# Splitting two of the 51 loads of a scan input into a 120-row and an 8-row transfer

## The chip, the cores and the metric

The kernel runs on one core of one Trainium2 chip. A core has five engines with instruction streams of their own: TensorE (PE in the profile; PEld is its weight load), VectorE (DVE), ScalarE (ACT), GpSimd (POOL) and SyncE (SP), which here does nothing but issue transfers. Transfers between HBM and the on-chip memory (SBUF, 128 rows called partitions) are carried out by 16 DMA engines. The metric is the device time of one execution in microseconds (us); the profile shows the span from the first to the last instruction of one execution, which is somewhat shorter than the device time.

## The reference, cut to what matters

`a` and `b` have shape (8, 6400, 128). A linear recurrence runs along the 6400 steps of each of the 8 sequences, and its result is the input of a mixture of eight low-rank adapters, of which each row uses the best two:

```python
def _attn_ref(a, b):                 # a, b: (8, 6400, 128) float32
    h = zeros((8, 128))
    for t in range(6400):
        h = a[:, t] * h + b[:, t]
        out[:, t] = h
    return out

def _moe_ref(x, w_gate, A, B):       # x: (51200, 128); 8 adapters of rank 16
    logits = x @ w_gate
    topk = the 2 largest of the 8 logits of each row
    w = softmax over these 2
    delta = sum over the 2 of  w * ((x @ A[e]) @ B[e])
    return x + delta
```

Nothing of `a`, `b` or the result can be left in HBM: 26.2 MB of `a`, 26.2 MB of `b` and 26.2 MB of the result pass the DMA engines once each.

## The kernel before

The 51,200 rows are cut into 100 units of 512 rows. For each unit PE transposes `a` and `b` into PSUM, ACT copies the transposed `a` to SBUF, and DVE runs the recurrence as one scan instruction into `xT`. PE then forms the gate logits and the rank-128 products of all adapters (`ZL`), ACT copies them out (`zl`), a chain of small steps on POOL, DVE and ACT computes the gate weights, POOL or DVE multiplies (`zw`), PE transposes back (`T`), applies the second factor and adds x (`D`), and ACT copies the unit to `outt` (`oev`), from where SP stores it. A planner in Python fixes the order of instructions on each engine at build time and sets the waits on semaphores.

A transfer is planned by `add_dma`. Each issue in `starts` adds 16 to the semaphore of its slot when it has landed, and a user waits for the sum of all of them:

```python
def add_dma(name, eng, unit, starts, slot, ns, deps=(), kind="dma", issue=450.0, after=2000.0):
    if slot not in dma_sem:
        dma_sem[slot] = [sb(nc.semaphore(...)), 0]
    dma_sem[slot][1] += 16 * len(starts)
    sem, value = dma_sem[slot]

    def emit(h):
        for dst, src in starts:
            last = h.dma_start(dst, src).then_inc(sem, 16)     # line 429
        return last

    add(name, eng, kind, unit, issue * len(starts), emit, deps, (sem, value, ns, after))
```

`a` and `b` have rings of 8 places in SBUF, and a place holds two units: 128 partitions of 8 consecutive rows of 128 numbers, so 4 KB in a partition and 512 KB in a load. Three loads at the start and one at the end hold one unit alone (256 KB). The place `n` of `a` holds the units 2n-1 and 2n.

```python
def load(t, w):
    n = place(t, w)[0]                       # a: (w + 1) // 2,  b: w // 2
    many = 1 if (t, w) in alone else 2
    dst, i = rings[t][:, n % RING, :], QI    # RING = 8, QI = 8
    ...
    src = rows_of[t][w * UT : (w + many) * UT, :].rearrange("(p i) d -> p (i d)", i=i)
    add_dma(
        f"ld{t}{w}", "sp", ...,
        [(dst, src)],                        # one transfer of 128 partitions
        (t, n % RING, many, w if many == 1 else 0),
        1290.0 if many == 2 else 690.0,
        users.get((t, n - RING), []),        # PE has read what the place held before
    )
```

A store takes two units as well (512 KB), except the first two and the last two. It waits for the two copies to `outt` and for the scan 20 units later; the ring `outt` has 24 units.

```python
def o_evac(v):
    ...                                       # ACT (the last 8 units: ACT or DVE)
    copy(outt[:, v % NOUT, :], bank(("O", v))[:, :])     # line 978; after D{v} and store of v - 24

stores = [(u, 2) for u in range(0, NU - 2, 2)] + [(NU - 2, 1), (NU - 1, 1)]
def store(j):
    ...
    add_dma(f"st{j}", "sp", u0 + HOLD, [(rows, tile)], ("o", s0, n), ns,
            [f"oev{v}" for v in range(u0, u0 + n)] + [f"scan{min(u0 + HOLD, NU - 1)}"])
```

All loads of `a` and `b` and all stores are issued by SP, one after the other, on one queue (q1 in the profile).

Of the kernel before, what the change touches and what calls it, by code (L numbers as in the profile page):

```python
# [10 lines left out]


CFG = {
    "ring": 8,
    "xr": 20,
    "zr": 48,
# [263 lines left out]
def bass_associative_scan_2x2__then__mixture_of_adapters_kernel(  # L280
# [18 lines left out]
    NU = N // UT  # L299
    RING = CFG["ring"]  # L300
    XR = CFG["xr"]
    NOUT = CFG["nout"]
    HOLD = CFG["hold"]
    NAS = CFG["ast"]
    NZW, NZT = 3, 3
    ZR = CFG["zr"]
    TAIL = CFG["tail"]
# [61 lines left out]
    with ExitStack() as stack:  # L369
# [50 lines left out]
        def add_dma(name, eng, unit, starts, slot, ns, deps=(), kind="dma", issue=450.0, after=2000.0):  # L420

            if slot not in dma_sem:
                dma_sem[slot] = [sb(nc.semaphore("q_" + "_".join(map(str, slot)))), 0]
# [5 lines that stand above are left out]
                    last = h.dma_start(dst, src).then_inc(sem, 16)  # L429
                return last  # L430

            add(name, eng, kind, unit, issue * len(starts), emit, deps, (sem, value, ns, after))
# [163 lines left out]
        def place(t, w):  # L596

            shift = 1 if t == "a" else 0
            half = 64 * ((w + shift) % 2)
            return (w + shift) // 2, slice(half, half + 64)  # L600
# [7 lines left out]
        def column(t, w):  # L608

            return w * UT if t == "b" else 0  # L610

        def load(t, w):

            n = place(t, w)[0]
            many = 1 if (t, w) in alone else 2
            dst, i = rings[t][:, n % RING, :], QI
            if many == 1:
                dst, i = dst[:, column(t, w) : column(t, w) + UT], Q
            src = rows_of[t][w * UT : (w + many) * UT, :].rearrange("(p i) d -> p (i d)", i=i)
            for k in range(many):  # L620
                load_of[t, w + k] = f"ld{t}{w}"
            add_dma(
                f"ld{t}{w}",
                "sp",
                w - 2 * RING + (0 if w > 3 else -200),
                [(dst, src)],
                (t, n % RING, many, w if many == 1 else 0),
                1290.0 if many == 2 else 690.0,
                users.get((t, n - RING), []),
            )  # L630
# [384 lines left out]
        for w in range(NU):  # L1015
            for t in "ab":
                if (t, w) not in load_of:
                    load(t, w)
# [71 lines left out]
```

## Time and profile before

| | before |
|---|---|
| device time, median of 3 runs | 201.62 us (201.49 to 201.7) |
| span of the profiled execution | 200.2 us |
| PE / ACT / DVE / POOL busy | 92% / 90% / 87% / 79% of the span |
| data moved | 79.30 MB, mean 396 GB/s |
| loads of a, loads of b, stores | 51 each, 49 of each with 512 KB |
| last store issued | 195.0 us |

How to read it. The times in the profile are microseconds from the span's start. An engine's share of busy time is an average over the span; what counts at the end is what the last instruction waited for. For a transfer the profile gives the time from its issue to its landing, in which it waits behind what was queued before it. Besides, the trace has a record for every increment that a transfer makes to its semaphore. A transfer of 128 partitions leaves 16 such records, at up to 16 different times; these are called its landing records below, sorted from the first to the 16th. The transfer has landed for its users only with the last.

### The profile page before, as it was taken

To read this page: it belongs to the slowest core of one execution; us is meant where nothing else is said; L and a number is where in the kernel's file an instruction comes from. 1 tells how busy PE (TensorE), PEld (TensorE's weight loads), DVE (VectorE), ACT (ScalarE), POOL (GpSimd) and SP (SyncE) were. 2 spreads that over 40 slices of the span, in tenths; PEclk is the share of its full clock that TensorE was granted. 3 is DMA by queue.
4 is the path that set the end of the run, shared out by engine and by line. 5 is a ranking of instruction groups with operands and counts; after the bars stand their busy time and mean duration, and the time that the engine had idled before them with its cause. 6 is when DMAs were issued, how large, how long until landed. Compare 5 with 4: busy or idle time off the path is not lost.

```text
span 200.2 us, 8009 instructions
## 1 busy us (share of the span) xinstructions
PE 184.2 (92%) x3202; PEld 163.2 (82%) x3202; DVE 173.8 (87%) x302; ACT 180.0 (90%) x463; POOL 158.5 (79%) x278
## 2 busy tenths in 40 slices
PE   7599899999999999999989999999999999897760
PEld 3478797899998989999979998898899898796650
DVE  3369999999999999899989889879797999789950
ACT  3159999999999999999999999999999999999770
POOL 2315658889898999988789999999999898887720
PEclk9759999999999999999999999999999999999998
DMA  5999999999999999999999999999999999998994
GB/s 204 352 417 408 410 405 406 408 402 410 403 420 413 414 417 418 413 414 420 410 416 413 414 413 414 421 413 417 418 413 415 413 416 413 412 369 328 407 383 172
DMA packets 22629, 79.30 MB, mean 396 GB/s; under 512 B 2624, under 2 KB 2880, under 8 KB 22592
## 3 DMA queue, kind: packets, MB, share of 16 engines
q1 hardware_dynamic: 22160, 78.65, 97.8%
q8 instruction: 25, 0.41, 0.8%
q10 hardware_dynamic: 432, 0.14, 0.3%
q14 instruction: 12, 0.10, 0.1%
HBM read 52.56 MB, written 26.21 MB: 393 GB/s over the span
## 4 chain that ended last, share of the span: by engine, by line
PE 56%; DVE 22%; ACT 9%; DMA 3%; issue 3%; POOL 3%; POOLq 1%; SPq 0%; DVEq 0%; ACTq 0%
PE ps L94 29%; PE ps L98 28%; DVE xT L710 17%; ACT outt L978 3%; DMA a_in<-in_a_dram 3%; ACT a_st L686 3%; DVE zwT L942 2%; ACT zl L767 2%; POOL zw L926 2%; POOLq L369 1%; POOL d L880 1%; ACT pn L816 1%; DVE zw L926 1%; DVE m L851 1%; DVE m L873 0%
## 5 line engine op out<-in xcount | busy, mean ns | idle before, releaser
L710 DVE TENSOR_TENSOR_SCAN xT<-a_st,xT,ps 128x512 f16<-128x512 f32 x96 | 120.3, 1253 | 12.6 <-PE ps L98 6.2
L926 POOL TENSOR_TENSOR zw<-zl,g 128x512 f16<-128x512 f32 x93 | 99.2, 1072 | 8.5 <-ACT g L905 6.8
L767 ACT COPY zl<-ps 128x408 f32<-128x408 f32 (+1 forms) x139 | 73.0, 532 | 1.6 <-PE ps L94 1.6
L98 PE MATMUL ps<-ident_f,a_in 64*128 64x64 f32 (+1 forms) x792 | 68.7, 232 | 2.2 <-DMA a_in<-in_a_dram 2.2
L98 PE MATMUL ps<-ident_f,b_in 64*128 64x64 f32 (+1 forms) x792 | 67.4, 231 | 0.1
L686 ACT COPY a_st<-ps 128x512 f32<-128x512 f32 x100 | 60.9, 628 | 7.2 <-PE ps L98 6.2
L98 PEld LDWEIGHTS ps<-ident_f,a_in 64*128 64x128 f32 (+1 forms) x792 | 57.5, 141 | 9.5 <-DMA a_in<-in_a_dram 2.7
L978 ACT COPY outt<-ps 128x512 f32<-128x512 f32 x100 | 60.9, 625 | 2.0 <-PE ps L94 1.3
L98 PEld LDWEIGHTS ps<-ident_f,b_in 64*128 64x128 f32 (+1 forms) x792 | 56.5, 141 | 1.2 <-DVE xT L710 0.4
L94 PE MATMUL ps<-cst_h,xT 128*128 128x136 f16 x400 | 51.3, 236 | 1.0 <-DVE xT L710 0.5
L94 PE MATMUL ps<-ident_h,xT 128*128 128x128 f16 x400 | 42.5, 229 | 1.3 <-DVE zwT L942 1.0
L98 PE MATMUL ps<-ident_h,zw 128*128 128x128 f16 x400 | 39.1, 220 | 4.3 <-DVE zw L926 2.0
L94 PEld LDWEIGHTS ps<-cst_h,xT 128*128 128x128 f16 x400 | 36.4, 148 | 6.0 <-DVE xT L710 2.5
L94 PE MATMUL ps<-cst_h,zwT 128*128 128x128 f16 x400 | 38.7, 220 | 0.0
L942 DVE COPY zwT<-ps 128x256 f32<-128x256 f32 x89 | 35.7, 409 | 2.6 <-PE ps L98 2.4
L94 PEld LDWEIGHTS ps<-ident_h,xT 128*128 128x128 f16 x400 | 33.0, 147 | 3.4 <-DVE zwT L942 2.5
L98 PEld LDWEIGHTS ps<-ident_h,zw 128*128 128x128 f16 x400 | 25.0, 98 | 8.4 <-POOL zw L926 3.2
L94 PEld LDWEIGHTS ps<-cst_h,zwT 128*128 128x128 f16 x400 | 27.2, 99 | 0.0
L816 ACT ACTIVATE pn<-d 128x96 f32<-128x96 f32 (+2 forms) x72 | 22.6, 322 | 0.9 <-POOL d L858 0.6
L888 POOL TENSOR_TENSOR d<-d 128x96 f32<-128x96 f32 (+2 forms) x36 | 13.8, 383 | 5.0 <-DVE d L841 4.6
L866 POOL TENSOR_TENSOR L<-zl,pn 128x96 f32<-128x96 f32 (+2 forms) x34 | 12.9, 380 | 5.1 <-ACT pn L816 4.9
L880 POOL TENSOR_TENSOR d<-zl,m 128x96 f32<-128x96 f32 (+2 forms) x34 | 12.2, 359 | 4.7 <-DVE m L873 4.7
(38 smaller groups left out, 90.0 us busy)
## 6 DMA issues: line engine op xcount, KB each, us to landing
a_in<-in_a_dram SPq DMA_DIRECT2D x49, 512.0 KB, 15.3
b_in<-in_b_dram SPq DMA_DIRECT2D x49, 512.0 KB, 15.3
out_dram<-outt SPq DMA_DIRECT2D x49, 512.0 KB, 15.3
a_in<-in_a_dram SPq DMA_DIRECT2D x2, 256.0 KB, 8.9
b_in<-in_b_dram SPq DMA_DIRECT2D x2, 256.0 KB, 4.8
out_dram<-outt SPq DMA_DIRECT2D x2, 256.0 KB, 4.7
cst_f<-in_moe_A_dram ACTq DMA_DIRECT2D x1, 64.0 KB, 3.5
cst_f<-in_moe_B_dram ACTq DMA_DIRECT2D x1, 64.0 KB, 6.2
```

Source lines behind the costliest of these rows:

```text
L94: return self.handle.matmul(*args, **kwargs)
L98: return self.handle.transpose(*args, **kwargs)
L686: lambda h: h.copy(a_st[w % NAS][:, :], bank(("a", w))[:, :]),
L710: last = h.tensor_tensor_scan(out=x_at(lo, hi), data0=a_st[w % NAS][:, lo:hi], data1=bank(("b", w))[:, lo:hi], initial=init, op0=ALU.mult, ...
L767: return h.copy(zl[:, r0 : r0 + n, :], src)
L816: lambda h: h.activation(v(pn[s]), v(src[s]), ACTF.Relu, bias=bias, scale=scale),
L866: lambda h: h.tensor_tensor(out=v(L2[s]), in0=Lg, in1=v(pn[s]), op=ALU.subtract),
L880: lambda h: h.tensor_tensor(out=v(d2[s]), in0=Lg, in1=bc(m2[s]), op=ALU.subtract),
L888: lambda h: h.tensor_tensor(out=v(d1[s]), in0=v(d1[s]), in1=v(d2[s]), op=ALU.add),
L926: lambda h: h.tensor_tensor(out=oview, in0=zview, in1=gview, op=ALU.mult),
L942: return copy(zwT[v % NZT][:, :].bitcast(F32), bank(("O", v))[:, 0 : UT // 2])
L978: return copy(outt[:, v % NOUT, :], bank(("O", v))[:, :])
```

## The change

Two of the 51 loads of `a`, those into place 4 (units 7 and 8) and into place 24 (units 47 and 48), are each made as two transfers, one of partitions 0 to 119 and one of partitions 120 to 127. The same bytes go to the same addresses. The name "fifteen" tells what it is for: 120 is 15 times 8, so that the rows of the large transfer divide over 15 DMA engines with 8 rows each, as before over 16, and the other 8 rows are shared out afresh.

```diff
 CFG = {
+    "fifteen": (("a", 4), ("a", 24)),
     "ring": 8,
...
                 f"ld{t}{w}",
                 "sp",
                 w - 2 * RING + (0 if w > 3 else -200),
-                [(dst, src)],
+                [(dst[r, :], src[r, :]) for r in ((slice(0, 120), slice(120, 128)) if (t, n) in CFG["fifteen"] else (slice(0, 128),))],
                 (t, n % RING, many, w if many == 1 else 0),
                 1290.0 if many == 2 else 690.0,
                 users.get((t, n - RING), []),
```

The order of instructions and the waits on PE, DVE, ACT and POOL are the same in both kernels. SP issues two transfers more (155 instead of 153); the 120-row transfer takes over the wait of the load that it replaces, and the 8-row transfer follows with no wait of its own. The semaphore of a split load rises by 32 instead of 16, and PE waits for all of it.

## The prediction

> **What bounds the kernel now.** I read the chain of waits first, from its end backwards, then the landing of the last transfers, then the table of waits, then the DMA part of the page. The chain of the last stretch ends with these pieces (start, length, what):
>
> ```profile
> 193.23 0.44 DVE zwT L942
> 193.67 0.05 issue
> 193.72 0.65 PE ps L94 x8
> 194.37 0.02 issue
> 194.39 0.59 ACT outt L978
> ```
>
> So the last computation is ACT's copy of the last unit, done at 194.98. The span is 200.2, and in the table of busy time by stretches (us of the stretch, then PE, PEld, DVE, ACT, POOL, then clock, DMA share and GB/s) nothing computes after 195:
>
> ```profile
> 190.00:195.00 5.00, 3.61 (x54) 2.92 (x51) 2.89 (x4) 3.98 (x9) 1.57 (x2) 1.00 0.96 381
> 195.00:200.00 5.00, 0.00 (x0) 0.00 (x0) 0.00 (x0) 0.00 (x0) 0.00 (x0) 0.86 0.48 190
> ```
>
> The last 5 us are the last store. The transfers issued after 185 show how long one takes from issue to landing:
>
> ```profile
> out_dram<-outt SPq DMA_DIRECT2D x6, 512.0 KB, 7.1
> out_dram<-outt SPq DMA_DIRECT2D x2, 256.0 KB, 4.7
> ```
>
> Is 4.7 us a latency or a queue? The landing records of the trace answer. Of the 16 increments of each of the last transfers I take the 1st, 8th, 15th and 16th:
>
> ```
> issued   1st     8th     15th    16th
> 185.81   190.56  190.66  191.61  193.30
> 188.63   193.13  193.25  194.10  195.93
> 191.35   194.40  194.50  196.48  197.18
> 193.68   196.13  196.25  197.71  198.43
> 195.00   197.50  197.59  198.95  199.68
> ```
>
> Fourteen engines or so land the last store at 197.5 to 197.9, 2.5 us after its issue. One engine lands at 198.95 and one at 199.68. The 16th column advances by 1.25 to 1.37 us for each 512 KB store from 179.8 on, without a pause: that engine still has a backlog, and the kernel's end is its end. The kernel is bound by computation up to 195.0 and after that by **one late DMA engine**.
>
> The engines drift apart during the kernel. The distance from the 1st to the 16th record is 1.6 us for the load of place 4 of a (14.45 to 16.05), 4.05 for that of place 24 (72.72 to 76.77) and 6.1 at 172. Each steps up when the instruction queues run; the page's DMA part says
>
> ```profile
> q1 hardware_dynamic: 22160, 78.65, 97.8%
> q8 instruction: 25, 0.41, 0.8%
> ```
>
> 0.8% of 16 engines' span is 25.6 us, some 1.0 us for each of 25 packets, and each packet sits on one engine.
>
> Does the computation wait for loads meanwhile? The longest rows of the table of waits (total, times, longest) that name a load are
>
> ```profile
> PEld ps L98 <- DMA a_in<-in_a_dram: 2.7, 1, 2.7
> PE ps L98 <- DMA a_in<-in_a_dram: 2.2, 1, 2.2
> ```
>
> each once, and both at the start. From the 16th landing of a load to PE's first use of it I find 0.2 to 2.2 us between 10 and 35 us, 4 to 8 around 50, and 2 to 5 from 80 on. The waits of the stretch from 9 to 40 us hold no row with a load in it. From 13 to 31 us the chain is DVE's scan, one after the other, not PE.
>
> [...]
>
> **The change part by part.**
>
> *Engine 15 loses work.* Its 8 packets of 4 KB in each split load go elsewhere. One load occupies an engine for 1.25 to 1.28 us (first records of loads queued one behind the other: 14.45, 15.72, 17.00). Two loads: 2 x 1.27 = 2.5 us less backlog. All engines are backlogged from 10 us to about 176 us (even the first record comes 8 us after the issue at 163), so this should be kept until the queues drain.
>
> *Engines 0 to 7 gain work.* One row each, twice: 2 x (1.27 / 8) = 0.32 us. Engines 8 to 14: nothing.
>
> *SP issues two transfers more*, for 0.4 to 1.1 us each (its issue durations in the timeline). From 10 to 164 us SP only follows the queue, landing 15.3 us behind; in the last 20 us, where SP issues stores as soon as ACT is done, nothing is added. Cost at the end: 0.
>
> *PE waits for one semaphore value as before*; the 8-row transfer follows directly and lands with the other one. Cost: 0.
>
> *The sum.* If the late engine is engine 15, its end moves from 199.68 to about 197.2, but then the next engine, at 198.95, ends the kernel: gain 199.68 - 198.95 = **0.73 us**, less up to 0.32 if that engine is one of 0 to 7. So 0.4 to 0.7 us. If the 15th engine were out of the way too, the limit would be the 197.5 of the others, a gain of 2.2 us.
>
> **The rivals.**
>
> 1. *The late engine is not engine 15.* Then its relief is nothing. If it is among 0 to 7[...], the end moves out by 0.32 us, to 201.9; if it is among 8 to 14, by nothing. For it: the records have no numbers, and fetches spread over engines. Against: the change exists for this one engine, and was set at just two loads, which fits a lead of the late engine (2.7 us at 191, 195.93 against 193.13) almost exactly.
> 2. *It is all hidden.* Loads land before their use and PE doesn't wait, so a load that lands earlier gives nothing; the work before 195.0 should stay as it is. I hold this to be true of the computation, and it is why the gain can't exceed the tail. If the tail also were latency only, the time would stay at 201.6. The 1st records at 197.5 speak against that.
> 3. *Relief feeds computation.* Between 17 and 31 us loads land as little as 0.2 us ahead of PE, and the 16th record is a whole microsecond behind the 15th (23.42 against 22.42). Were this on the path, splitting the load of place 4 could bring up to 1 us more. Against: DVE is back to back there.
> 4. *The split transfers are slow ones.* [...]a costlier issue for 15 engines, could delay two loads by a microsecond or so. With 1.8 us between the landing of place 4 and its use and 3.8 at place 24, that would be hidden, or at worst give back half a microsecond.
>
> **Range and chances.** Late engine is 15: 60%, time near 201.62 - 0.6 = 201.0. Late engine is another: 40%, time 201.6 to 201.95. Weighted 0.6 x 201.0 + 0.4 x 201.75 = 201.3; I put the point a little to the side of the likelier branch, at 201.1 us. The range is 200.5 (the relieved engine and the second both earlier) to 201.9 (rival 1 with the added rows). A change of 2% is 4 us. The tail after the last issue is only 4.7 us long and half of that is there on every engine, so 2% either way is all but excluded: faster 0.01, same 0.98, slower 0.01.
>
> **What would show it.** Landing records of the two split loads: 15 and 8 of the 16 increments late, the rest at once[...]. The gap between the 1st and 16th record at 191 should fall from 2.8 us to about 1, and the last record of the last store should come at 3.8 to 4.3 us after its issue instead of 4.7. The last copy by ACT should stay at 194.4 within 0.3. The prediction is wrong if the last copy moves (then the computation did feel the loads, or the queues drained differently), or if the 16th column keeps its lag (rival 1), or if the instruction fetch at 193.5, which put the 15th record back by 1.1 us, falls on another engine.

## The result and the profile after

| | before | after |
|---|---|---|
| device time, median of 4 runs | 201.56 us | 204.41 us (204.19 to 204.69) |
| ratio | | 1.0146, 95% interval 1.0124 to 1.0169 |
| span of the profiled execution | 200.2 us | 202.5 us |
| last store issued | 195.0 us | 195.44 us |
| last store landed, last of its 16 records | 199.68 us | 201.79 us |

The change makes the kernel slower by 1.5%, some 2.9 us, where I had expected 0.5 us less.

The engine numbers of the prediction are names, as no record bears one: 15 is the engine that the 120-row transfer leaves out, 0 to 7 are the eight of the 8-row transfer. That 15 is none of these eight was my assumption. The split load of place 4 left 25 landing records where a whole load leaves 16: two at once (5.60 and 6.05 us) and 23 from 15.30 to 17.28 us, of 15 engines and of 8. The first of the 23 comes 2.49 us after the first record of the load before (12.81), about what 8 packets of 312 ns take.

The end of the chain of waits, after (start, length, what):

```profile
193.95 0.65 PE ps L95 x8
194.60 0.02 issue
194.62 0.59 ACT outt L979
```

The last copy by ACT starts at 194.62 instead of 194.39. Nearly all of the difference between these two executions lies behind it, in the last transfers. The busy times by stretches (PE, PEld, DVE, ACT, POOL, clock, DMA share, GB/s), and the transfers issued after 185:

```profile
195.00:200.00 5.00, 0.00 (x0) 0.00 (x0) 0.00 (x0) 0.21 (x1) 0.00 (x0) 0.70 0.62 245
200.00:202.00 2.00, 0.00 (x0) 0.00 (x0) 0.00 (x0) 0.00 (x0) 0.00 (x0) 0.50 0.04 16
```

```profile
out_dram<-outt SPq DMA_DIRECT2D x6, 512.0 KB, 9.0
out_dram<-outt SPq DMA_DIRECT2D x2, 256.0 KB, 6.5
```

A last store now takes 6.5 us to land instead of 4.7. The landing records say why; the last three stores of the changed kernel:

```
issued   1st     8th     15th    16th
193.92   196.39  197.12  198.68  200.54
194.58   197.05  197.76  199.29  201.17
195.44   197.74  198.40  199.92  201.79
```

The late engine is still there, and it is later: 4.05 us behind the first one on the last store, where it was 2.18.

Where did it lose that time? The same stretch of both kernels, around the split load of place 4, first before and then after:

```profile
13.00:16.00 3.00, 2.87 (x51) 2.10 (x47) 2.52 (x3) 2.60 (x8) 1.37 (x3) 0.79 1.03 415
```

```profile
13.00:16.00 3.00, 1.90 (x35) 1.56 (x32) 2.55 (x3) 1.53 (x5) 0.70 (x3) 1.00 1.01 218
```

The last two numbers are the ones to read. The DMA engines are busy all the time in both (share 1.0), yet after the change they move 218 GB/s instead of 415. Busy is not moving. The DMA view of that stretch counts the packets: 341 before, and after

```profile
DMA packets 183, 0.66 MB, mean 218 GB/s; under 512 B 23, under 2 KB 23, under 8 KB 183
```

So a packet takes about twice as long. The packet records of the trace agree: over the whole execution 4 KB packets take 159 ns at the median before and after, but 312 to 313 ns between 13 and 15 us of the changed kernel, with single ones up to 459 there and 506 by 18 us. Around the split load of place 24 (75 to 76 us) the median is 275 ns.

To put a number on it I use **extra packet time**: over the 4 KB packets of a stretch, the sum of what each took above 159 ns, divided by 16 engines. From 12 to 18 us it is 0.09 us before and 1.79 us after; from 72 to 78 us it is 0.05 and 0.95. Together 2.7 us per engine, close to the 2.9 us lost.

PE now waits for loads in the early part as well. The chain from 5 to 22 us runs through a load of b, and the table of waits (total, times, longest) has rows that the kernel before had not (of b there is only one, of 0.2 us):

```profile
5.92 12.79 DMA b_in<-in_b_dram
18.71 0.14 issue
18.85 1.22 PE ps L99 x19
```

```profile
PE ps L99 <- DMA b_in<-in_b_dram: 1.4, 2, 1.1
PEld ps L99 <- DMA b_in<-in_b_dram: 1.2, 1, 1.2
```

This is the load of b that is issued right after the split one; it landed at 17.34 before and lands at 18.71 now.

### The profile page after: what moved, and what is told of

Same layout as the page of the kernel before. It is cut to its first block, busy times and chain, and to the rows that moved or that the text cites. A ratio compares the mean times of both kernels' runs of the same rounds, so it can differ in the third digit from the quotient of the medians.

```text
span 202.5 us, 8011 instructions
## 1 busy us (share of the span) xinstructions
PE 184.0 (91%) x3202; PEld 163.8 (81%) x3202; DVE 174.0 (86%) x302; ACT 179.9 (89%) x463; POOL 158.6 (78%) x278
## 4 chain that ended last, share of the span: by engine, by line
PE 56%; DVE 13%; ACT 12%; DMA 6%; issue 3%; POOL 2%; SPq 2%; POOLq 1%; DVEq 0%; ACTq 0%
PE ps L99 28%; PE ps L95 28%; DVE xT L711 10%; DMA b_in<-in_b_dram 6%; ACT outt L979 4%; ACT a_st L687 4%; ACT zl L768 3%; SPq L430 2%; DVE zwT L943 2%; POOL zw L927 2%; POOLq L370 1%; ACT pn L817 1%; ACT g L906 1%; POOL d L881 1%; POOL um L896 0%
## 5 line engine op out<-in xcount | busy, mean ns | idle before, releaser
L99 PE MATMUL ps<-ident_f,a_in 64*128 64x64 f32 (+1 forms) x792 | 69.5, 230 | 2.0 <-DMA a_in<-in_a_dram 2.0
L95 PE MATMUL ps<-cst_h,xT 128*128 128x136 f16 x400 | 50.7, 235 | 0.7 <-DVE xT L711 0.5
L896 POOL TENSOR_TENSOR um<-d,pn 128x96 f32<-128x96 f32 (+2 forms) x36 | 14.2, 395 | 3.3 <-ACT pn L817 1.9
```

Source lines behind the costliest of these rows:

```text
L95: return self.handle.matmul(*args, **kwargs)
L99: return self.handle.transpose(*args, **kwargs)
L896: lambda h: h.tensor_tensor(out=v(um[s]), in0=v(d1[s]), in1=v(pn[s]), op=ALU.subtract),
```

## The experiments

Theory P, a conjecture: the split transfers put several engines on the same part of SBUF at one time, which makes packets slow for everyone. Rivals: the second issue and semaphore cost (I), fifteen engines or uneven shares cost (F), or only one of the two places matters. Which engine writes which row no record shows, as none bears an engine number. So the runs can only vary which partitions a transfer writes, and compare the length of its packets.

**The second issue alone.** Edit: the loads are cut by columns.

```diff
-[(dst, src)],
+[(dst[:, c], src[:, c]) for c in ((slice(0, 512), slice(512, 1024)) if (t, n) in CFG["fifteen"] else (slice(None),))],
```

> The same two loads are each made as two transfers of 128 partitions, one with the first 2 KB and one with the second 2 KB of each partition. Same number of issues, same doubled semaphore, all 16 engines[...]. Theory P ([...]engines write into the same part of SBUF at the same moment and every packet takes twice as long): nothing of that here, 4 KB packets become 2 KB packets of 84 ns, time 201.4 to 201.9. Theory I (the second issue and the second semaphore of a load cost the time): 203.5 to 204.5 as with the change.

Measured: ratio 0.9997 (0.9982 to 1.0012). Two issues and a semaphore of 32 cost nothing that shows. Theory I is out.

**All sixteen engines, two halves.** Edit: `slice(0, 64), slice(64, 128)` in place of 120 and 8.

> The same two loads as two transfers of 64 partitions each: 16 engines[...] in both, so no engine is relieved and none gets more. Theory P: packets take some 310 ns while these two loads run, as in the changed kernel, each load costs every engine about 1.25 us more, and the end moves to 204 to 204.8 us. Theory F (the cost comes from fifteen engines instead of sixteen, or from the uneven shares): packets at 159 ns, time as before, 201.3 to 202.

Measured: 1.0143 (1.0069 to 1.0216), as much as the change. Its four runs fall into two pairs, 203.61 and 203.99, 206.25 and 206.28 us, so that it loses is clear and how much is not. Extra packet time 1.43 us at place 4 and 0.83 at place 24, the median packet 311 ns at 13 us. Each half left 16 landing records; no engine was relieved and none got more, so theory F is out too.

**One place at a time.** Edit: `"fifteen": (("a", 4),)`, then `(("a", 24),)`.

> Only the load of place 4 is split 120 and 8. Theory P with a late engine that is not engine 15: the late engine loses 1.25 us at this load and never gets idle time to make it up, so the end moves by 1.0 to 1.4 us, to 202.6 to 203.0. If instead the early loads matter because PE waits for them (the records show loads landing up to 1.4 us later between 17 and 32 us), this run alone has most of the loss, 203.5 or more, and the other place has little.

> Only the load of place 24 is split 120 and 8. Theory P with a late engine that is not engine 15: 1.0 to 1.4 us more, 202.6 to 203.0, the same as for place 4, with loads landing well before their use in this part. If the early loads matter: 201.6 to 202.2. In the landing records, if engine 15 is the one that is late at 76 us, the 16th record of the loads just after the split loses its distance of 1.0 us to the 15th; if it is not, the distance stays.

Measured: 1.0100 (1.0077 to 1.0124) for place 4 and 1.0046 (1.0029 to 1.0064) for place 24. They add up to the 1.0146 of the change. I had expected the two to be equal, with 202.6 to 203.0 us; they aren't, and place 4 alone took 204.19 (median). The extra packet time is 1.82 us for place 4 and 0.74 for place 24, and the losses are 2.0 and 0.9 us. The two rivals within theory P (all in the tail, or nearly all early) were both too simple. Of place 24 the loss seems to be in the tail: ACT's last copy starts at 193.47 there and the last store takes 5.9 us to land. Of place 4 it reaches the computation: in that profile ACT's last copy starts at 195.77. One such start says little, though. In seven profiles of kernels that do the same up to 59 us (the kernel before, and the runs that change only place 24 or 49) it lies anywhere from 191.79 to 194.39, and the last store lands between 198.88 and 200.90: the tail takes up much of the difference. 195.77 is clearly outside that range.

**The same time on the engines without slow packets.** Edit: no split; the load of the place is followed by one more of the same 512 KB into a spare tile that nobody reads (`n` is 4 or 24).

```diff
+h.dma_start(spare[:, :], src).then_inc(q_spare, 16)      # right after the load of place n; SP's last instruction waits for it
```

> No load is split. Right after the load of place 4 its 512 KB are loaded once more, into a spare tile that nobody reads: 8 usual packets of 159 ns on each of the 16 engines, so 1.27 us more for every engine at that point, with no slow packets, no doubled semaphore and no uneven shares. Theory P says that the split of place 4 costs nothing but such time on the engines: 203.0 to 204.3 us, as with place 4 split alone (1.010 of before). If something else in the split of place 4 costs (its own late landing, the 8-row rest), this run loses clearly less, 0 to 1 us.

> The same extra 512 KB load after the load of place 24. Theory P: as with place 24 split alone (1.0046 of before), 202.4 to 203.2 us, with the last copy by ACT not moved and the last store landing about 1.2 us later after its issue than before. If a mid-kernel load really is hidden and the split of place 24 costs by its shape: 201.5 to 202.

Measured: 1.0060 (1.0046 to 1.0074) and 1.0062 (1.0047 to 1.0077), or 1.2 us for 1.27 us of packets on each engine, at either place (at place 4 the median of 202.66 us is under the 203.0 to 204.3 that I expected). So here a microsecond of DMA time on every engine costs about a microsecond of kernel, early or late. For place 4 the split costs more than the extra load because it takes more time on the engines (1.82 us), and for place 24 less (0.74).

The run with the extra load at place 24 is the kernel before up to 60 us, and its profile has a lesson. There, PE does wait for an early load, and the chain from 5 us runs through it:

```profile
PE ps L98 <- DMA b_in<-in_b_dram: 1.4, 1, 1.4
```

```profile
5.53 11.60 DMA b_in<-in_b_dram
17.27 1.01 PE ps L98 x19
```

In the profile I predicted from, the first loads had landed late (7.71 us for the second load of a, 5.9 in the changed kernel), the scans started late, and the loads after that seemed to have time.

**Is the late engine the relieved one?** Edit: `"fifteen": (("a", 49),)`, the last full load of a.

> Only the last 512 KB load of a (place 49, issued near 157 us) is split 120 and 8; after it only stores follow, and the engines that are not late run dry near 180 us and make up what they lost. If the engine that is late at the end is engine 15, it is relieved by 1.27 us, and the end comes earlier by 0.4 to 0.9 us: 200.8 to 201.3. If it is one of 0 to 14, it loses 1.2 us and never runs dry: 202.5 to 203. The first is what the prediction assumed, the second is what the landing records of the split of place 24 point to (the distance from the 15th to the 16th record stayed).

Measured: 1.0063 (1.0040 to 1.0086). It is not: the late engine lost time instead of gaining. The landing records show that one engine was relieved: on a store of the queue after the split (issued at 165.97) the first record is 0.82 us ahead of the second, where a load issued at 139.6 had 0.07. The relieved engine jumped to the front. The 16th was 0.2 us behind the 15th on the first load after the split (issued at 158.74) and 1.0 us on that store: nothing relieved it.

**Extra work for eight engines.** Edit: after the load of place 24 two transfers of 8 partitions with 16 KB each.

```diff
+for j in range(2):
+    h.dma_start(spare[j:32:4, :], rows_of["a"][256 * j : 256 * (j + 1), :].rearrange("(p i) d -> p (i d)", i=32)).then_inc(q_spare, 16)
```

> After the load of place 24, 256 KB more go to a spare tile in two transfers of 8 partitions of 16 KB each, four partitions apart[...]. If the late engine is among 0 to 7: as in the run with the extra 512 KB after place 24, 202.4 to 203.2. If it is among 8 to 15: 201.5 to 202.1, with half of the engines late by 1.2 us in the landing records and the 16th unmoved.

Measured: 1.0069 (1.0046 to 1.0092), the same as the extra load over all sixteen. The two transfers left 18 records, 8 each and one each at once: eight engines took part. In equal shares that is 32 KB on each, as much as a 512 KB load puts on each of 16. So the late engine is one of these eight (0 to 7 in the expectation). Whether they are the eight of the change's 8-row transfers was not shown.

The landing records add something that I had overlooked. The engine that is late at this moment is not one of the eight: the 16th record is 3.24 us behind the first just before the extra transfers and 3.20 just after, and their last record comes at 75.67 us, before the 16th of the load ahead of them (75.77). So the sign that I had set for engines 8 to 15, an unmoved 16th record, came as well, from an engine that was passed later. The engine that ends the kernel falls behind later, and with stores: from 66 to 176 us of this run the 16th record advances by 1.41 us with a store and 1.25 with a load (medians of 32 and 49), the first record by 1.28 and 1.22. In the kernel before, from 153 to 192 us, the 16th record advances by 1.36 us with a store against 1.24 with a load. So the late engine loses some 0.1 us with every store; why is open. Followed back by these steps it lies 1.5 us behind the first record just before the extra transfers, where the records near it (74.02 and 74.04 us) are followed by records of the extra transfers 0.61 and 0.62 us later: it is one of the eight, as the ratio of 1.0069 says.

**Pieces of sixteen partitions.** Edits, at place 24: `slice(16 * j, 16 * j + 16) for j in range(8)`, and `slice(j, 128, 8) for j in range(8)`.

> The load of place 24 is made as eight transfers of 16 neighbouring partitions[...]. By theory P[...] packets up to 620 ns, and the load costs every engine 2 to 3.7 us more: 203.5 to 205.3 us. If the number of transfers or uneven shares cost and not the placing: as in the run with step 8 beside it, whatever that is.

> The load of place 24 is made as eight transfers of 16 partitions that lie 8 apart: the same number of transfers, issues, engines and packets as in the run with 16 neighbouring partitions, but the 16 engines write to partitions spread over the whole of SBUF[...]. Theory P: packets of at most some 310 ns, 0.7 to 1.3 us more for every engine: 202.2 to 202.9 us, clearly under the run beside it. If it is the number of transfers: both alike.

Measured: 1.0007 (0.9996 to 1.0018) and 0.9995 (0.9980 to 1.0009). A miss: the losses that I had derived from theory P (2 to 3.7 us and 0.7 to 1.3 us) didn't come. Extra packet time was only 0.43 and 0.12 us from 71 to 78 us. So theory P doesn't describe these transfers, or where rows land isn't all.

**Only the base partition differs.** Edit: after the load of place 4, its bytes once more in two transfers of 64 partitions, with `lo` 0 or 32.

```diff
+for j in range(2):
+    h.dma_start(spare[lo:lo + 64, 1024 * j : 1024 * (j + 1)], src[64 * j : 64 * (j + 1), :]).then_inc(q_spare, 16)
```

> No load is split. Right after the load of place 4 its 512 KB are loaded once more, as two transfers of 64 partitions into partitions 0 to 63 of a spare tile, 4 packets for each of 16 engines in each. The two runs with sixteen partitions at a time left theory P in doubt: they [...]lost nothing. Theory P: [...]packets of some 310 ns as with the split into halves, and 1.2 us more than the run beside it: 203.4 to 204.4 us. If it isn't where the rows land but the size or shape of the transfer: the same as the run beside it.

> The same two extra transfers, of the same bytes of HBM by the same engines, but into partitions 32 to 95 of the spare tile. [...]Theory P: packets stay at 159 ns, and the run loses what the extra 512 KB load after place 4 lost (1.006 of before): 202.3 to 203.1 us. If the shape of the transfer costs (64 partitions[...]): slow packets as in the run beside it, 203.4 to 204.4.

Measured: 1.0145 (1.0094 to 1.0195) into partitions 0 to 63 and 1.0061 (1.0037 to 1.0084) into 32 to 95. From 16 to 19 us, first the low partitions, then the middle ones:

```profile
16.00:19.00 3.00, 1.19 (x19) 0.92 (x19) 2.42 (x5) 1.99 (x6) 1.70 (x4) 1.00 1.02 194
```

```profile
16.00:19.00 3.00, 0.51 (x15) 0.54 (x15) 2.22 (x4) 0.74 (x3) 0.57 (x3) 1.00 1.02 410
```

The DMA share is 1.02 in both; 194 GB/s against 410. Same bytes, same number of transfers, all 16 engines busy in both, and the partitions alone decide: packets of 296 to 395 ns (medians of each microsecond from 15 to 19 us) against 159 to 164 ns. The second run loses what a whole extra load loses (1.0061 against 1.0060). That where a transfer lands in SBUF can double its packets is thus shown; that several engines meet on one part there is still a conjecture. For the 120-row transfer itself the cause is carried over from here and from the two halves: no run moved its 120 rows to other partitions.

**The pieces of sixteen where the engines are in step.** The same two edits as above, at place 4.

> The load of place 4 as eight transfers of 16 neighbouring partitions each. At place 24 this lost nothing (1.0007). If that was because the engines are 3 to 4 us apart there: here they are within 1 to 2 us,[...] and packets take 400 to 620 ns, 2 to 4 us lost: 203.5 to 205.5.[...]

> The load of place 4 as eight transfers of 16 partitions that lie 8 apart[...]. If it is a matter of engines in step: packets of some 310 ns and 1 to 2 us lost, 202.6 to 203.6, less than with 16 neighbouring partitions beside it. If [...]one packet at a time is always absorbed: packets of some 160 ns, 201.3 to 202.

Measured: 1.0096 (1.0067 to 1.0124) and 1.0058 (1.0036 to 1.0080), with extra packet time of 1.53 and 1.18 us. Here both cost. Neighbours cost more than rows 8 apart, as I had expected from theory P, but the two intervals overlap, and the packets of neighbours are not slower: the largest medians of a microsecond are 289 ns for neighbours and 291 for rows 8 apart, not the 400 to 620 that I had expected of neighbours (an estimate of up to twice the 312 ns of the change). So the direction of the loss fits theory P and the size doesn't. What spared the same pieces at place 24 is in the situation there. On the transfer just before the pieces the 16th record is 4.5 and 3.2 us behind the first at place 24, and 2.1 and 0.6 us at place 4 (neighbours, then 8 apart). That the pieces cost only where the engines are close together in time fits theory P; this distance was not varied by itself.

The losses beside the added time per engine (extra packet time, plus 1.27 us where 512 KB were added; losses are ratio minus 1, times 201.5 us). The stretches are those named above, 12 to 19 us for the extra 64 partitions and 162 to 174 us for place 49. The added time is that of one execution, which need not be a typical one: that of the low partitions took 206.01 us, that of the two halves 203.61.

| run | added per engine, us | lost, us |
|---|---|---|
| the change | 1.79 + 0.95 = 2.7 | 2.9 |
| two halves | 1.43 + 0.83 = 2.3 | 2.9 (1.4 to 4.4) |
| place 4 / place 24 / place 49 split | 1.82 / 0.74 / 1.03 | 2.0 / 0.9 / 1.3 |
| extra load at 4 / at 24 | 1.27 / 1.27 | 1.2 / 1.2 |
| extra 64 partitions, low / middle | 1.27 + 2.44 = 3.7 / 1.27 + 0.16 = 1.4 | 2.9 (1.9 to 3.9) / 1.2 |
| neighbours at 4 / step 8 at 4 | 1.53 / 1.18 | 1.9 / 1.2 |
| neighbours at 24 / step 8 at 24 | 0.43 / 0.12 | 0.1 / -0.1 |

## Why the prediction was wrong

**The tail of one late engine.** Right. The end is that engine's end in both kernels, and the distance moved from 2.18 to 4.05 us. DMA time added to all engines showed up nearly in full (1.2 us for 1.27). Two readings were a little off: the 16th column advances by 1.25 to 1.41 us from 179.8 on, not 1.25 to 1.37, and the first record after the issue at 163 comes 9.0 us later, not 8.

**"Engine 15 loses work", 2.5 us.** The relief itself took place: the records of the runs with a split show one engine at the front afterwards, 0.8 us ahead at place 49 and 1.34 after both places. By the step "the late engine is engine 15: 60%", my estimate, for which the kernel before has no record, this should have helped. The step failed: the late engine is another one, by the run with place 49 split (1.0063), and one of the eight that took the extra work (1.0069). That was rival 1, which I had at 40% with a loss of at most 0.32 us.

**"Engines 0 to 7 gain work" 0.32 us, "engines 8 to 14: nothing".** This is the step that failed by its size, and the one that decided the sign of the result. It took the 1.27 us of a usual load for the split one. The packets of the split load and of those beside it kept each engine, on average of the 16, busy for 1.79 us longer at place 4 and 0.95 at place 24: 2.7 us for the two places instead of 0 to 0.32. Rival 4 had named slow split transfers, and then called them hidden, or half a microsecond at worst.

**"It is all hidden" and rival 3.** The loads before about 30 us are not hidden. The slack of 0.2 to 2.2 us came from one execution with a late start. In the profile of the change PE waits for them, and in the profile with place 4 split alone the last copy comes 1.4 us later than in the one profile that I had. Rival 3, that loads are on the path early, was right in mechanism with the sign turned round: the loads came later, not earlier.

**Issue and semaphore at no cost.** Right: 0.9997 with the loads cut by columns.

**What was to show it.** A split load leaves 23 late records, as 15 and 8 engines should, and 2 at once. The distance of the 16th record at 191 was to fall from 2.8 to 1 us and rose to 4.7 (store issued at 187.90). The last copy was to stay within 0.3 us, and did in the profile of the change (0.23); that was partly chance, as its range in like kernels is 2.6 us wide, and the change's early loads started sooner and then lost it again (the load two before the split one landed at 12.41 instead of 13.50 us, the next one at 14.89 instead of 14.78). The instruction fetch before the end (the last 16 KB packet of q8, at 193.97 us, 0.96 us long) put back the 15th record again (193.74 to 196.23 us, stores issued at 187.90 and 188.87) and not the 16th.

## What to carry to other kernels

Before a transfer is cut by partitions, measure what the new ones do to its packets: here 64 neighbouring partitions from 0 ran at half speed (194 GB/s) and the same number from 32 at full speed (410 GB/s), and in the changed kernel the load behind the slow transfer landed later (18.71 us instead of 17.34). A DMA share of 1.02 stood beside both rates; read GB/s or the length of packets with it. One late DMA engine ended this kernel (199.68 us before, 201.79 after), and it was not the one that the change relieved: find out which it is before work is taken from another. And slack that one profile shows at the start of a kernel is to be looked at in a second one: where one showed 0.2 to 2.2 us of it, another had PE wait 1.4 us for a load.

## What the runs showed of the hardware that I had not expected

- 4 KB packets went from 159 ns to medians of 296 to 395 ns by the base partition of a 64-partition transfer alone (0 instead of 32).
- One transfer of 15 engines and one of 8 left 25 semaphore records instead of 32: one for each engine, and one more for each transfer right after its issue (5.60 and 6.05 us for issues at 4.98 and 5.51), which by the sum carries the rest.
- A load that nobody reads, 512 KB or 0.66% of the bytes, cost 0.60% to 0.62% of the time, though the compute engines of the kernel before are 79% to 92% busy.
